# A list schedule's due times, leads and planned lengths are set anew, and five late low halves lie at other addresses

## The chip, the cores and the metric

The kernel runs on one core of one Trainium2 chip. The metric is the device time of one execution in microseconds (us). PE is TensorE (matmul), DVE is VectorE, ACT is ScalarE, POOL is GpSimd, SP is SyncE, which here only issues DMAs.

## The reference

Banded attention over 4 batches, 8 heads, 768 positions and 64 features per head (each position sees the 128 positions up to its own and the first 4), and behind it a feed-forward layer without experts to choose from:

```python
def _attn_ref(q, k, v, n_sink, window):
    scores = (1.0 / np.sqrt(D)) * np.matmul(q, k.transpose(0, 1, 3, 2))
    keep = (pos[None, :] < n_sink) | ((rel >= 0) & (rel < window))      # n_sink 4, window 128
    scores = np.where(keep, scores, -1000000000.0)
    a = np.exp(scores - np.max(scores, axis=-1, keepdims=True))
    a = a / (np.sum(a, axis=-1, keepdims=True) + 1e-09)
    return np.matmul(a, v)

def _moe_ref(x, w_in, w_out):            # x: 3072 x 512, w_in: 512 x 2048, w_out: 2048 x 512
    h = x @ w_in
    g = h - np.tanh(h)
    return g @ w_out
```

All inputs are fp32. The kernel keeps fp32 accuracy by splitting an operand into a high half (rounded to fp32r, which TensorE takes) and a low half (what the rounding left), and adding the products high by high, low by high and high by low.

## The kernel before

**Tiling.** The 3072 tokens are 12 chunks of 256 tokens, the 2048 columns of `w_in` are 8 groups `g` of 256. A pair of chunk and group is a step `n`; there are 96. Steps 0 to 23 are chunks 0 to 2, mixed; from there on step 24 + 8(c − 3) + g is group `g` of chunk `c`, so that a chunk is eight steps in a row. A step is one block of 24 matmuls 128x256 (`mm1`, L823, into `h`), a gate, and a second half. The gate is a tanh on ACT (L843), a difference on DVE (L846), and the split into a high half on ACT and a low half on DVE: L849 (`ghbuf`) and L852 (`glbuf`) in the steps before 40, and L862 and L865, with three more sums on DVE (L857 to L859), from step 40 on. The second half multiplies by `w_out`: 12 matmuls 128x512 at L894 (eight on the high half of the gate, four on the low one), or, in steps 40 to 94, 21 matmuls 128x256 at L928, which are the three passes over seven Strassen products. Their weights (`edge`, and a block in `w`) are made on the chip.

**Attention** is cut into 48 units, four pairs of heads for each chunk. A unit is: scores on PE (L532 in the first chunks, L539 after), the mask and its row maximum on DVE (L554, L556), exponentials on ACT (L564), reciprocals on DVE (L584, L585), scaling on ACT (L590), three small operations for the first four positions on POOL (L599 to L601, `z`), transposes on PE (L624 of `p`, L665 of `z`), merges on DVE (L638), and the products with `v` on PE (L681, L687). The next unit's `q` and `k` are split on ACT and DVE (L508, L511, L497, L502). What comes out is split into `xall` (L704, L708), the operand of `mm1`.

**Weights for the Strassen steps.** `derive(g, m)` makes a sum of two blocks of `w_out`: SP copies the one into place (L1023), POOL starts a DMA that adds the other to it (L1026), ACT rounds the sum to its high half (L1029), DVE leaves the low half (L1036, or L1034 for a negative sum). For `m` = 1, 3, 4 the sum goes into an `edge` tile, in the time of chunk 3's attention; for `m` = 6 it goes into `w` itself, group by group in steps 32 to 39, as soon as the last plain second half has read that block.

**Other DMAs.** The blocks of `w_in` are kept in device memory and streamed back from step 24 on (L808, SP). POOL issues the loads of `q` and `k` (L370, L361) and half of the stores of the result (L985); SP issues the other half.

**What sets the order.** All of this is handed as tasks to a list schedule, `Work`. A task names its engine, a planned length (`took`), a due time, and what it reads and writes; a DMA names in `lands` how long until its data are there. `order()` plays the tasks through, always takes the ready task with the earliest due time, and the instructions are written out in the order that comes out. Each engine then runs its own queue in that order, and waits at an instruction whose inputs aren't there. Due times are made of `due_step(n)` (FIRST, EARLY, PACE) and leads: LEAD3 for chunk 3's attention, LEAD for later chunks, DEAR and DLATE for `derive`, WLEAD and WNEXT for the weights. LAND is added to a DMA's landing:

```python
free[e], done[n] = t + (took if e == "POOL" else lands), t + lands + (1700 if self.all[n][2] < self.late else self.land)
```

Nothing but these numbers decides where in an engine's queue an instruction stands.

**Where low halves lie.** `low7(n)` puts the low half of a Strassen step into a flat buffer, at an offset that is zero but for the steps in a table (`ASIDE`, in words of four bytes; a product's block is 128 words):

```python
def low7(n):
    a = ASIDE.get(n, 0)
    return glflat[:, a : a + 7 * P].rearrange("p (b t) -> p b t", b=7)
```

Of the kernel before, what the change touches and what calls it, by code (L numbers as in the profile page):

```python
# [233 lines left out]
def _banded(tc, qd, kp, vp, vs, small, masks, w_in, w_out, ident, pts, early, out):  # L234
    nc = tc.nc
    et = mybir.EngineType
    with ExitStack() as ctx:
# [16 lines left out]
        banks = {n: ps.tile([P, 512], F32, tag=n, name=n) for n in ("s0", "s1", "o0", "o1", "t", "x")}  # L254
# [9 lines left out]
        kscr = dpool.tile([2, P, 2, DM // 2], F32, tag="kscr", name="kscr")  # L264

        RAW, TWO, CUT, DUO, SC, PB, ZL, TK = 12, 12, 2, 3, 4, 4, -4000, 1100
        SLK, PAD, LATE, LAND, QP, KP, BP, LEAD3 = 0.0, 1.05, 65222.0, 4372.0, 0, 0, 0, 89032.0
        SA, NSLOT, RING, GP, LQ, ST = 5, 7, 7, 0, 1, 1
        work = Work(SLK, PAD, LATE, LAND)

# [4 lines left out]
        order += [(cc, g) for g in range(CUT, NG) for cc in (2, 1)] + [(0, g) for g in range(CUT, NG)]  # L275
        order += [(cc, g) for cc in range(3, NCHUNK) for g in range(NG)]
        NS = len(order)
        FIRST, EARLY, PACE, LEAD = 45000.0, 4600.0, 8242.0, 72963.0
        UNIT, SECOND, WLEAD, WNEXT = 2000.0, 3000.0, 6000.0, 2500.0
        HALF2, LAST = 8269.0, 4401.0  # L280
        SPILL, STREAM, DEAR, DLATE = 54590.0, 4000.0, 39769.0, 31275.0

        def due_step(n):
            return FIRST + EARLY * min(n, 24) + PACE * max(0, n - 24)
# [20 lines left out]
        def shift(n):  # L305
            return SHIFT if n < 24 else 0

        ASIDE = {81: 48, 85: 104, 89: 84, 92: 60}

        def low7(n):  # L310
            a = ASIDE.get(n, 0)
# [624 lines left out]
        def second_half7(n):  # L936
            cc, g = order[n]
            if closes(n):
                runs = [[(m, k) for m in ms for k in range(3)] for ms in ((4, 3), (1,), (2, 5), (7, 6))]
            else:  # L940
                runs = [[(m, k) for m in ms for k in range(2)] for ms in ((4, 3), (1,), (2, 5), (7, 6))]
                runs += [[(m, 2) for m in ms] for ms in ((4, 3, 1), (2, 5, 7, 6))]
            for run in runs:
                def some(run=run):
                    for m, k in run:
                        mm7(n, m, k)

                r = []
                for m, k in run:
                    r.append(("gl", 0) if k == 2 else ("gh", n % 2))  # L950
                    r.append(("e", g, m) if m in (1, 3, 4) else ("w", 1, g))
                banks = {where7[m] for m, _ in run}
                work.add("PE", 119 * len(run), due_step(n) + HALF2, some, sorted(set(r), key=str), sorted(banks))
            if closes(n):
                gather(n)

# [56 lines left out]
        def derive(g, m):  # L1013
# [32 lines left out]
                else:  # L1046
                    src.append(("edge", e))
            took = 300 * n
            work.add("SP", 400, d, copied, src, w + old, lands=took + 100)
            work.add("POOL", 650, d, added, src, w, lands=1000 + 600 * n)  # L1050
            work.add("ACT", 360 * n, d, rounded, (), w)
            work.add("DVE", 360 * n, d, rest_of, (), w, port=True)

# [13 lines left out]
        def first_half(n):  # L1067
            cc, g = order[n]
            if streamed(n):
                for j in range(4):  # L1070
                    work.add("SP", 500, due_step(n) - STREAM + 700 * j, lambda j=j: stream(n, j),
                             [("scr", g, j // 2)], [("ring", ring_at(n, j))] + ([("w", 0, 1)] if cc == 3 and g == 0 else []), lands=850)
            for f in range(2):
                for z in range(2):
                    def some(k0=f * 12 + z * 6):
                        for k in range(k0, k0 + 6):
                            mm1(n, k)

                    x = [("xu", home(cc), 2 * z), ("xu", home(cc), 2 * z + 1), ("x", home(cc))]
                    w = ("ring", ring_at(n, 2 * f + z)) if streamed(n) else ("w", 0, g)  # L1080
                    work.add("PE", 722, due_step(n) - LAST * (n == NS - 1), some, x + [w], [("h", n % 2)])

        def second_half(n):
            if strassen(n):
# [295 lines left out]
```

## Time and profile before

| | |
|---|---|
| device time, three runs | 682.92, 680.07, 674.58 us; median 680.07 |
| the profiled execution | 675.38 us, of it 673.6 from the first to the last instruction |
| busy, of the span | PE 97%, DVE 81%, ACT 59%, POOL 24% |
| mean granted TensorE clock | 0.997 of full |
| instructions | 14515, of them 5099 matmuls |

The three runs spread over 8.3 us, and the profiled execution is near the fastest of them. Matmuls overlap, so that a row of x24 is 24 matmuls that start evenly in the time to the next row's start; a row's own duration reaches into the next.

### The profile page before, as it was taken

The page shows a single profiled execution, that of the slowest core. Times are in us where ns is not written, and L with a number is a line of the kernel's source. Part 1 is how long each engine was busy: PE and PEld are TensorE (multiplying, and loading weights), DVE is VectorE, ACT ScalarE, POOL GpSimd, SP SyncE. Part 2 cuts the span into 40 slices and gives each one's busy share as a digit, 9 for nine tenths or more (in the row PEclk, how much of TensorE's full clock was granted, in tenths as well). Part 3 has the DMA queues.
Part 4 walks back from the last instruction along what each step waited for, and adds up shares of the span by engine and source line. Part 5 has one row for each costly group of instructions (what it writes and reads, how often), then busy time and mean ns, then how long its engine had stood idle before and what let it go on. Part 6 is the DMA issues. An engine that isn't in the chain of part 4 may idle for free.

```text
span 673.6 us, 14515 instructions
## 1 busy us (share of the span) xinstructions
PE 650.5 (97%) x5099; PEld 601.6 (89%) x5099; DVE 543.8 (81%) x1397; ACT 395.8 (59%) x1024; POOL 163.5 (24%) x331
## 2 busy tenths in 40 slices
PE   6899999999999999998999999999999999999995
PEld 4677899989879899897999999899999999999995
DVE  6899998965999877576799899888999889855654
ACT  5986443435887767555675666667566567523331
POOL 5444000002863242232412212222212211100100
PEclk9999999999999999999999999999999999999998
DMA  5878797785989676899977767766776866656861
GB/s 174 282 253 284 271 302 252 290 289 160 217 198 268 205 221 219 241 271 279 253 250 239 222 210 219 240 199 193 238 231 192 263 208 194 216 152 199 260 195 37
DMA packets 79342, 152.97 MB, mean 227 GB/s; under 512 B 9564, under 2 KB 25564, under 8 KB 79260
## 3 DMA queue, kind: packets, MB, share of 16 engines
q1 hardware_dynamic: 65884, 121.65, 57.3%
q0 software_dynamic: 13376, 30.30, 16.4%
q8 instruction: 42, 0.69, 0.4%
q14 instruction: 40, 0.33, 0.2%
HBM read 131.47 MB, written 20.45 MB: 226 GB/s over the span
## 4 chain that ended last, share of the span: by engine, by line
PE 78%; DVE 7%; DMA 4%; ACT 4%; issue 3%; POOL 3%; SPq 0%; POOLq 0%; DVEq 0%; ACTq 0%
PE h L823 32%; PE s L928 10%; PE o L928 8%; PE o L894 7%; PE x L687 3%; PE s L894 3%; PE t L687 2%; DMA w<-bscr 2%; PE t L624 2%; PE t L894 2%; PE x L894 2%; PE t L539 2%; PE x L539 2%; PE s L539 1%; DMA v<-vp 1%
## 5 line engine op out<-in xcount | busy, mean ns | idle before, releaser
L823 PE MATMUL h<-xall,ring 128*128 128x256 f32 x990 | 127.6, 278 | 0.0
L823 PEld LDWEIGHTS h<-xall,ring 128*128 128x128 f32 x990 | 120.1, 188 | 0.9 <-DMA ring<-wscr 0.2
L843 ACT ACTIVATE gbuf<-h 128x512 f32<-128x512 f32 x96 | 57.3, 596 | 98.2 <-PE h L823 71.4
L823 PE MATMUL h<-xall,spare 128*128 128x256 f32 x738 | 96.2, 278 | 0.0
L862 ACT CAST ghbuf<-gbuf 128x896 fp32r<-128x896 f32 x55 | 51.9, 943 | 66.4 <-DVE gbuf L859 66.3
L823 PEld LDWEIGHTS h<-xall,spare 128*128 128x128 f32 x738 | 89.9, 188 | 0.6 <-issue 0.2
L370 POOL DMA_DIRECT2D qraw<-qd x36 | 27.5, 764 | 229.2 <-DVE q L511 181.1
L865 DVE TENSOR_TENSOR glbuf<-gbuf,ghbuf 128x896 fp32r<-128x896 f32 x55 | 59.8, 1088 | 18.8 <-ACT ghbuf L862 16.5
L564 ACT ACTIVATE p<-p,st 128x132 f32<-128x132 f32 x132 | 52.5, 400 | 11.3 <-DVE st L556 10.3
L894 PE MATMUL o<-w,ghbuf 128*128 128x512 f32 x192 | 51.0, 399 | 0.3 <-ACT ghbuf L849 0.3
L846 DVE TENSOR_TENSOR gbuf<-h,gbuf 128x512 f32<-128x512 f32 x55 | 37.8, 688 | 15.2 <-ACT gbuf L843 14.4
L823 PE MATMUL h<-xall,w 128*128 128x256 f32 x384 | 49.3, 279 | 0.0
L823 PEld LDWEIGHTS h<-xall,w 128*128 128x128 f32 x384 | 47.3, 188 | 1.5
L502 DVE TENSOR_TENSOR ks<-kraw,ks 64x392 fp32r<-64x392 f32 x72 | 40.4, 561 | 6.1 <-ACT ks L497 4.0
L590 ACT ACTIVATE p<-p,st 128x132 f32<-128x132 f32 x132 | 42.6, 395 | 4.0 <-DVE st L585 3.6
L894 PEld LDWEIGHTS o<-w,ghbuf 128*128 128x128 f32 x192 | 33.7, 188 | 6.4 <-ACT ghbuf L849 0.8
L497 ACT CAST ks<-kraw 64x392 fp32r<-64x392 f32 x72 | 37.1, 515 | 3.8 <-DMA kraw<-kp 2.9
L846 DVE TENSOR_TENSOR h<-h,gbuf 128x512 f32<-128x512 f32 x41 | 28.5, 696 | 12.8 <-ACT gbuf L843 12.2
L638 DVE TENSOR_TENSOR pt<-t,below 128x512 f32<-128x512 f32 (+1 forms) x48 | 28.8, 599 | 10.7 <-PE t L624 5.7
L928 PE MATMUL o<-w,ghbuf 128*128 128x256 f32 x220 | 35.7, 281 | 0.0
L928 PE MATMUL s<-edge,ghbuf 128*128 128x256 f32 x220 | 35.6, 280 | 0.0
L928 PE MATMUL s<-w,ghbuf 128*128 128x256 f32 x220 | 35.1, 278 | 0.0
(180 smaller groups left out, 1537.7 us busy)
## 6 DMA issues: line engine op xcount, KB each, us to landing
ring<-wscr SPq DMA_DIRECT2D x165, 256.0 KB, 4.5
spare<-wscr SPq DMA_DIRECT2D x123, 256.0 KB, 4.5
qraw<-qd POOLq DMA_DIRECT2D x36, 256.0 KB, 5.1
wraw<-w_in SPq DMA_DIRECT2D x16, 512.0 KB, 6.1
wraw<-w_out SPq DMA_DIRECT2D x16, 512.0 KB, 6.6
wscr<-w SPq DMA_DIRECT2D x16, 512.0 KB, 6.4
kraw<-kp POOLq DMA_DIRECT2D x36, 196.0 KB, 4.3
v<-vp POOLq DMA_DIRECT2D x18, 256.0 KB, 3.7
```

The source lines that it names most:

```text
L497: nc.scalar.copy(ks[u][r, h, :], kt[u][r, :])
L502: (nc.gpsimd if KP else nc.vector).tensor_tensor(k[o, h, :], t[r, :], k[r, h, :].bitcast(F32), op=ALU.subtract)
L539: nc.tensor.matmul(ps[h][:, :WIN], lhsT=q[:, h, t * P : (t + 1) * P], rhs=rhs, start=i == 0, stop=i == 1,)
L564: nc.scalar.activation(e, e, AF.Exp, bias=st[u][:, j : j + 1], scale=-1.0, accum_out=st[u][:, 4 + j : 5 + j],)
L590: nc.scalar.activation(pr[u][:, j, :], pr[u][:, j, :], AF.Copy, scale=s[:, 8 + j : 9 + j])
L823: nc.tensor.matmul(hps[n][:, f, :], lhsT=w, rhs=x, start=r == 0, stop=r == 11)
L843: nc.scalar.activation(g0, h(), AF.Tanh)
L846: nc.vector.tensor_tensor(g0 if strassen(n) else h(), h(), g0, op=ALU.subtract)
L862: nc.scalar.copy(ghbuf[:, n % 2], gbuf[:, 1:, :])
L865: nc.vector.tensor_tensor(low7(n), gbuf[:, 1:, :], ghbuf[:, n % 2].bitcast(F32), op=ALU.subtract)
L894: nc.tensor.matmul(sums_of(n, cc, t), lhsT=a[:, f, t * P : (t + 1) * P], rhs=wt[1, g][:, (0, 1, 0)[i], f, :], start=first and not low and ...
L928: nc.tensor.matmul(acc, lhsT=a[:, b, :], rhs=factor(g, m, part % 2), start=g == 0 and part == 0 and m in (4, 1, 2, 7), stop=closes(n) and ...
```

## The change

Only numbers change. Seventeen of them are due times, leads and the like in the schedule's setting; four more are the landing times planned for the two DMAs of `derive` and the planned lengths of the blocks of matmuls at L823 and L928. They add and remove no instruction; what they change is the order in which engines get them. `ASIDE` changes addresses alone: before, steps 81, 85, 89 and 92 lay at 192, 416, 336 and 240 bytes from the buffer's start; now steps 81, 83, 86, 89 and 92 lie at 336, 240, 336, 240 and 336.

```diff
@@ -264,7 +264,7 @@
-        SLK, PAD, LATE, LAND, QP, KP, BP, LEAD3 = 0.0, 1.05, 65222.0, 4372.0, 0, 0, 0, 89032.0
+        SLK, PAD, LATE, LAND, QP, KP, BP, LEAD3 = 0.0, 1.05, 68932.8, 4939.1, 0, 0, 0, 92253.7
@@ -275,10 +275,10 @@
-        FIRST, EARLY, PACE, LEAD = 45000.0, 4600.0, 8242.0, 72963.0
-        UNIT, SECOND, WLEAD, WNEXT = 2000.0, 3000.0, 6000.0, 2500.0
-        HALF2, LAST = 8269.0, 4401.0
-        SPILL, STREAM, DEAR, DLATE = 54590.0, 4000.0, 39769.0, 31275.0
+        FIRST, EARLY, PACE, LEAD = 45488.2, 4498.8, 8248.4, 74582.8
+        UNIT, SECOND, WLEAD, WNEXT = 2182.8, 6399.4, 6045.8, 1426.5
+        HALF2, LAST = 8288.8, 5144.0
+        SPILL, STREAM, DEAR, DLATE = 62388.8, 3653.6, 44193.8, 26553.2
@@ -305,7 +305,7 @@
-        ASIDE = {81: 48, 85: 104, 89: 84, 92: 60}
+        ASIDE = {81: 84, 83: 60, 86: 84, 89: 60, 92: 84}
@@ -950,7 +950,7 @@
-                work.add("PE", 119 * len(run), due_step(n) + HALF2, some, sorted(set(r), key=str), sorted(banks))
+                work.add("PE", 123.7 * len(run), due_step(n) + HALF2, some, sorted(set(r), key=str), sorted(banks))
@@ -1046,8 +1046,8 @@
-            work.add("SP", 400, d, copied, src, w + old, lands=took + 100)
-            work.add("POOL", 650, d, added, src, w, lands=1000 + 600 * n)
+            work.add("SP", 400, d, copied, src, w + old, lands=took + 552)
+            work.add("POOL", 650, d, added, src, w, lands=2054 + 600 * n)
@@ -1078,7 +1078,7 @@
-                    work.add("PE", 722, due_step(n) - LAST * (n == NS - 1), some, x + [w], [("h", n % 2)])
+                    work.add("PE", 739, due_step(n) - LAST * (n == NS - 1), some, x + [w], [("h", n % 2)])
```

With LAND, the planned time from the issue of a `derive(g, 6)` copy to its landing goes from 700 + 4372 = 5072 ns to 1152 + 4939 = 6091 ns, that of its addition from 2200 + 4372 = 6572 to 3254 + 4939 = 8193 ns.

The order moves at these places of which the rows tell. In names such as `h_3649` the number is the program's count of tiles and differs between the two kernels for the same thing.

**Steps 39 and 40, ACT.** `h_3649` before and `h_3653` now are the first product of step 39, `h_3722` and `h_3732` that of step 40, `w_4` is the block of group 4 that `derive(4, 6)` makes, `p_3737` and `p_3713` are the same attention unit. Before:

```order
L1029 ACTIVATE w_3_1213<-w_3_1213 128x512
L590 ACTIVATE p_3591<-p_3591,st 128x132 x4
L843 ACTIVATE gbuf<-h_3649 128x512
L1029 ACTIVATE w_4_1330<-w_4_1330 128x512
L849 CAST ghbuf<-h_3649 128x512
L564 ACTIVATE p_3737,nswi<-p_3737,nswi 128x132 x2
L843 ACTIVATE gbuf<-h_3722 128x512
```

Now:

```order
L1029 ACTIVATE w_3_1193<-w_3_1193 128x512
L843 ACTIVATE gbuf<-h_3653 128x512
L849 CAST ghbuf<-h_3653 128x512
L564 ACTIVATE p_3713,nswi<-p_3713,nswi 128x132 x2
L508 CAST q_3743<-qraw_3636 128x512
L1029 ACTIVATE w_4_1298<-w_4_1298 128x512
L564 ACTIVATE p_3713,nswi<-p_3713,nswi 128x132 x2
L497 CAST ks_3772<-kraw_3687 64x392 x2
L590 ACTIVATE p_3713<-p_3713,nswi 128x132 x4
L843 ACTIVATE gbuf<-h_3732 128x512
```

The rounding of `w_4` stood ahead of the gate's high half (L849); now it stands behind it, behind the first two of the unit's exponentials (L564), and ahead of the other two, which the scaling (L590) needs.

**The same place, PE.** `t` and `x` are the two banks into which the scores (L539) go, `o` is the sum of the second half. Before, and then now:

```order
L539 MATMUL t<-ks_3628,q_3626 128x260 x2
L539 MATMUL x<-ks_3628,q_3626 128x260 x2
L823 MATMUL h_3722<-xall,ring 128x256 x18
L823 MATMUL h_3722<-xall,spare 128x256 x6
L539 MATMUL t<-ks_3628,q_3626 128x260 x2
L539 MATMUL x<-ks_3628,q_3626 128x260 x2
L894 MATMUL o_252<-w_7_1603,ghbuf 128x512 x4
```

```order
L894 MATMUL o_252<-w_6_1522,glbuf 128x512 x2
L894 MATMUL o_253<-w_6_1522,glbuf 128x512 x2
L539 MATMUL t<-ks_3638,q_3620 128x260 x2
L539 MATMUL x<-ks_3638,q_3620 128x260 x2
L823 MATMUL h_3732<-xall,ring 128x256 x18
L823 MATMUL h_3732<-xall,spare 128x256 x6
L894 MATMUL o_252<-w_7_1597,ghbuf 128x512 x4
L894 MATMUL o_253<-w_7_1597,ghbuf 128x512 x4
L624 MATMUL t<-ident,p_3713 128x128 x4
L894 MATMUL o_252<-w_7_1597,glbuf 128x512 x2
```

The second pair of scores stood behind the block of 24 matmuls; now it stands ahead of it, and behind the block comes, after eight matmuls of L894, the transpose (L624) of that unit's `p`.

**Steps 20 and 21, DVE.** `h_1991` before and `h_1988` now are the first product of step 21, `p_2158` and `p_2147` the same unit of chunk 3's attention. Before:

```order
L638 TENSOR_TENSOR pt<-t,below 128x4x128
L638 TENSOR_TENSOR pt<-t,after 128x4x128
L554 COPY_PREDICATED s_250<-above,s_250 128x128
L556 ISA p_2158,nswi<-s_250,mask 128x132
L556 ISA nswi 128x1
L554 COPY_PREDICATED s_251<-above,s_251 128x128
L556 ISA p_2158,nswi<-s_251,mask 128x132
...
L852 TENSOR_TENSOR glbuf<-h_1991,ghbuf 128x512
L511 TENSOR_TENSOR q_2189<-qraw_2113,q_2189 128x512
L584 TENSOR_SCALAR nswi<-nswi 128x4
```

Now:

```order
L511 TENSOR_TENSOR q_2086<-qraw_2005,q_2086 128x512
L502 TENSOR_TENSOR ks_2095<-kraw_2030,ks_2095 64x392 x2
L584 TENSOR_SCALAR st<-st 128x4
L585 RECIPROCAL st<-st 128x4
L852 TENSOR_TENSOR glbuf<-h_1988,ghbuf 128x512
L1034 SCALAR_TENSOR_TENSOR edge_1802<-edge_1802 128x256
L554 COPY_PREDICATED s_250<-above,s_250 128x128
L556 ISA p_2147,nswi<-s_250,mask 128x132
L556 ISA nswi 128x1
L554 COPY_PREDICATED s_251<-above,s_251 128x128
L556 ISA p_2147,nswi<-s_251,mask 128x132
```

The low half of step 21 (L852) stood behind both groups of that unit's masks (the group shown here is the second) and the merges L638 between them; now it stands ahead of all of them.

**POOL at 430 us.** `z` are the three operations for the first positions, `out` the store of a finished chunk. Before, and then now:

```order
L601 CAST z<-z 128x2x16
L985 DMA out<-wide 128x512
L985 DMA out<-wide 256x1x256
L599 CAST z<-p_5169 128x2x8
L600 TENSOR_TENSOR z<-p_5169,z 128x2x8
L601 CAST z<-z 128x2x16
L370 DMA qraw_5278<-qd 128x2x256
L361 DMA kraw_5326<-kp 128x392
```

```order
L370 DMA qraw_5186<-qd 128x2x256
L599 CAST z<-p_5123 128x2x8
L600 TENSOR_TENSOR z<-p_5123,z 128x2x8
L601 CAST z<-z 128x2x16
L985 DMA out<-wide 128x512
L985 DMA out<-wide 256x1x256
L361 DMA kraw_5299<-kp 128x392
```

The two stores stood ahead of `z`; now they stand behind it. The same exchange is made once more, at the unit whose `z` runs at 586 us.

## Rows read from the trace of the kernel before

**Rows 1.** The page: busy time of PE and DVE, and the granted clock by fortieths.
```profile
PE 650.5 (97%) x5099; PEld 601.6 (89%) x5099; DVE 543.8 (81%) x1397; ACT 395.8 (59%) x1024; POOL 163.5 (24%) x331
PEclk9999999999999999999999999999999999999998
```

**Rows 2.** Waits of PE: who waited for what, us in total, times, longest.
```profile
PE t L539 <- DVE nswi L556: 2.5, 1, 2.5
...
PE t L894 <- ACT ghbuf L849: 1.6, 2, 0.9
PE o L894 <- DVE glbuf L852: 1.6, 2, 1.3
...
PE x L665 <- POOL z L601: 0.8, 2, 0.6
```

**Rows 3.** Windows of 40 us: length, busy of PE, PEld, DVE, ACT, POOL, clock, DMA share, GB/s.
```profile
160.00:200.00 40.00, 38.12 (x279) 33.31 (x278) 35.71 (x114) 32.09 (x98) 28.47 (x44) 1.00 0.93 209
...
280.00:320.00 40.00, 37.48 (x251) 33.94 (x250) 27.16 (x77) 22.73 (x63) 12.02 (x20) 1.00 0.99 276
...
400.00:440.00 40.00, 39.37 (x357) 38.01 (x356) 36.51 (x96) 25.77 (x64) 10.32 (x21) 1.00 0.73 235
```

**Rows 4.** Timeline of PE at 318 us: start, us, instruction, idle before and releaser.
```profile
318.60 0.51 PE L539 MATMUL t<-ks,q 128*128 128x260 f32 x2 [2.48 <-DVE nswi L556]
```

**Rows 5.** Timeline of ACT from there.
```profile
315.94 0.63 ACT L1029 ACTIVATE w<-w 128x512 fp32r<-128x512 f32 x1 [5.63 <-DMA w<-bscr]
...
320.51 0.52 ACT L497 CAST ks<-kraw 64x392 fp32r<-64x392 f32 x1
320.93 0.40 ACT L564 ACTIVATE p<-p,nswi 128x132 f32<-128x132 f32 x1
...
323.86 1.30 ACT L590 ACTIVATE p<-p,nswi 128x132 f32<-128x132 f32 x4
```

**Rows 6.** DMA issues of `derive(g, 6)`: count, KB, median us from issue to landing.
```profile
w<-bscr SPq DMA_DIRECT2D x8, 256.0 KB, 4.8
w<-bscr POOLq DMA_DIRECT2D x8, 256.0 KB, 8.0
```

**Rows 7.** Timeline: the issues for group 4, on SP and on POOL.
```profile
299.45 0.37 SPq L1023 DMA_DIRECT2D w<-bscr  x1
307.93 1.22 POOL L1026 DMA_DIRECT2D w<-bscr  x1 [8.93 <-PE h L823]
```

**Rows 8.** Timeline of PE and DVE: low half of step 21, then that of 24.
```profile
187.76 1.20 PE L894 MATMUL o<-w,glbuf 128*128 128x512 f32 x4 [1.30 <-DVE glbuf L852]
187.02 0.69 DVE L852 TENSOR_TENSOR glbuf<-h,ghbuf 128x512 fp32r<-128x512 f32 x1
208.56 0.69 DVE L852 TENSOR_TENSOR glbuf<-h,ghbuf 128x512 fp32r<-128x512 f32 x1
210.16 2.02 PE L894 MATMUL o<-w,ghbuf 128*128 128x512 f32 x8
```

**Rows 9.** Timeline of POOL and PE at 430 us.
```profile
429.25 1.27 POOL L985 DMA_DIRECT2D out<-wide  x2 [8.40 <-DVE wide L980]
431.55 0.44 PE L665 MATMUL x<-ident,z 128*128 128x128 f32 x2 [0.63 <-POOL z L601]
```

**Rows 10.** The chain that ended last, late steps: start, us, what.
```profile
600.88 2.83 PE h L823 x24
606.18 2.83 PE h L823 x24
...
643.12 2.72 PE h L823 x24
648.22 2.72 PE h L823 x24
```

**Rows 11.** Timeline: the high half of step 48, and PE's first use of it.
```profile
376.08 0.95 ACT L862 CAST ghbuf<-gbuf 128x896 fp32r<-128x896 f32 x1
377.66 0.62 PE L928 MATMUL s<-edge,ghbuf 128*128 128x256 f32 x4
```

## The prediction

> **What bounds the kernel now.** The page comes first: PE is busy for 97% of the span, DVE for 81%, and the granted clock is full but at the end [rows 1]. So the time is PE's work, which this change leaves as it is, plus the moments in which PE stands still, plus the pace at which PE takes matmuls. The list of PE's waits tells what there is to win [rows 2]: 2.5 us once for scores that wait for a mask on DVE, 3.2 us for the high and low halves of gates, 0.8 us for POOL's `z`. The rest of PE's idle time is start and tail, and in both the order stays: the first seven gates have the same DVE work ahead of them, and the last hundred instructions of PE, DVE and ACT are the same. The windows say in which stretch the waits lie [rows 3]: 160 to 200 us, where DVE works 35.7 of 40 us, and 280 to 320, where DVE works only 27.2 of 40 but the DMA share is 0.99. The first stretch is short of DVE, the second waits for a transfer. In the window of 400 to 440 DVE is at 36.5 of 40: there the next bound lies close.
>
> **Part 1: the stall at 316 us.** After the block of step 40 PE starts the next scores at 318.60, with 2.48 us idle ahead of them [rows 4]. Behind it stands ACT, held until 315.94 by the DMA that adds into `w` [rows 5]; in DVE's queue the low half of that weight waits for ACT, and the gate's low half and the masks wait behind it. The copy was issued at 299.45, the addition at 307.93 [rows 7], so copy and addition took 315.94 − 299.45 = 16.5 us, where the medians of the eight are 4.8 and 8.0 [rows 6]. The new order takes the gate and the first masks out from behind the weight, so this wait of 2.5 us goes. What is late next? ACT now does, after the addition has landed: the weight (0.63 us, of which the next instruction overlaps some 0.1), the other two exponentials (each some 0.4 with a read behind it, 0.9 together), two casts of 0.52, and the scaling, 1.30 [rows 5]; then the transpose L624 can start. That is 0.5 + 0.9 + 1.0 + 1.3 + 0.2 for the signal = 3.9 us behind the landing, or 0.2 + 16.5 + 3.9 = 20.6 us behind the end of the pass that frees the block. In the new order PE has between that pass and this transpose 72 matmuls of 256 columns at 2.72/24 = 0.113 us [rows 10], 36 of 512 columns at twice that, 16 scores at 0.12 and four short ones: 8.2 + 8.2 + 1.9 + 0.3 = 18.6 us. If this transfer is as slow as before, 2.0 of the 2.5 us come back as a wait in front of the transpose: 0.5 us is won. If copy and addition take their medians (14.1 us with the 1.3 us that now lie between the copy's landing and the addition's issue, an estimate), none comes back: 2.5 us. The bounds are 0.5 and 2.5; I take 0.8, near the lower, since the row is of this very transfer and the DMA share of the stretch, 0.99 [rows 3], gives no reason for a quicker one.
>
> **Part 2: the gates of chunk 3's attention.** PE waits there twice for a low half, the longer time until 187.76 [rows 8], and once for a high half; from the starts of its matmuls the three cost 2.4 us. At 187.02 DVE starts on the half that PE wants [rows 8], and its row shows no idle time ahead: it wasn't waiting for data, it came late from its queue. Multiplying each row of the order by the mean time of such a row in the trace, DVE has 3.4 us less ahead of the low half of step 20 and 4.8 us less ahead of step 21's, and PE's work ahead of both is the same. The longest of these waits is 1.3 us [rows 2], so all of them should go: 2.4 us. The work isn't gone; it stands ahead of step 24 now, with 2.7 us more on DVE and 0.9 more on PE. There the low half was ready at 208.56 + 0.69 = 209.25, and PE came to it behind eight matmuls that began at 210.16 [rows 8], at 0.23 each: 2.8 us later. With PE 2.4 us earlier, 2.7 − 0.9 + 2.4 = 4.2 us would be asked for, if DVE never found time to catch up: up to 1.4 us of new wait for the low half. DVE has about 4.3 us free in the 40 [rows 3], so I take 0.9 of it. Sum of the part: 1.5 us, between −0.5 (step 24 late by more than counted) and 2.4.
>
> **Part 3: POOL's stores.** At 429.25 POOL starts two stores, 1.27 us long, then does `z`, and PE, which had waited 0.63 us for it, goes on at 431.55 [rows 9]. With `z` ahead of the stores, the issues fall away in front of it, more than PE's wait. The like holds at 586 us with 0.2 us. Matmul starts put the two waits at 1.16 us; I take the 0.8 of the list [rows 2]. The stores go out 1 us later, and nobody reads them. If `z` then waits for `p` on ACT, the win is nothing: 0 to 1.2 us.
>
> **Part 4: the addresses.** With the clock full, PE has two paces in the last 80 us. Steps with nothing but 24 + 21 matmuls follow each other every 606.18 − 600.88 = 5.30 us, and later every 648.22 − 643.12 = 5.10 us; their blocks of 24 take 2.83 and 2.72 us [rows 10]. The slow pace begins with the low half of step 81 (at 192 bytes from the buffer's start) and ends with that of step 89 (336 bytes); step 92's (240 bytes) is slow itself, and the pace after it is full. Eight steps at 0.20 us make 1.6 us. The change keeps just the two offsets after which the pace was full. Should they keep it so throughout, 1.6 us are won; should each such step merely turn the pace over, then steps 81 to 83, 86 to 89 and 92 to 95 are slow, eight again, and nothing is won; should all steps from 81 on be slow, 14 × 0.2 = 2.8 us are lost in place of 1.6: −1.2. I take 1.0, nearer to the first, because 336 and 240 bytes were each followed by the full pace the one time they occur, while no row shows them after a full pace.
>
> Here a rule speaks against the change. The Trainium skill, "SBUF — State Buffer", "Who interferes with whom", gives PE a read port for the moving operand and one for the weights, and says that PE never waits on anyone there; by it an address would move nothing. The trace has two paces at one clock, which that rule alone doesn't explain, and doesn't show that the address is their cause. By the rule the sum would be 1.0 us smaller.
>
> **Part 5: the rest.** From 340 to 595 us units and gates are interleaved anew. Counted as in part 2, DVE's work ahead of the gates of steps 41 to 64 grows against PE's by 1.4 to 2.7 us, and by 4.5 at step 48. The schedule sends PE to a gate just when it is ready: step 48's high half ends at 377.03 and PE uses it at 377.66, 0.63 us later [rows 11]. Where DVE has its results early the growth costs nothing; I take 0.4 us of new waits, between 0 and 4.
>
> **Sum.** 0.8 + 1.5 + 0.8 + 1.0 − 0.4 = 3.7 us less than the profiled execution of 675.38: 671.7, a ratio of 0.9945. The profiled execution lies 4.7 us under the median of the runs, 680.07; the forecast is for a median, so 680.07 × 0.9945 = 676.4 us.
>
> **The rivals.**
> *The waits only move.* The transfer of group 4 comes back in full as a wait of the transpose, step 24 is late by 1.4 us, and the pace turns over as before: 0.5 + 1.0 + 0.8 − 2 from part 5 = about 0.3 us, 679.8. For it speaks that three of the five parts have the next late thing in sight; against it that parts 2 and 3 win on engines that the rows show late by their own queue.
> *The address is nothing* (the skill's rule above): as forecast without part 4, 2.7 us, which gives 677.4.
> *DVE becomes the bound behind 340 us.* The place is step 48. If DVE, at 36.5 of 40 us in such a stretch [rows 3], has no time in hand, PE waits 4.5 − 0.6 = 3.9 us there, and with the 1.4 us of step 24 in full and the slow pace kept from step 81 on (−1.2) the sum is 0.8 + 1.0 + 0.8 − 1.2 − 3.9 = −2.5 us: 682.6, slower than before. It decides from the point where DVE is more than 4 us later at that gate than its slack. Against it: DVE's idle tenths are spread over the stretch, and one wait of PE gives all later gates the same time.
> *Everything works*: 2.5 + 2.4 + 1.2 + 1.6 = 7.7 us, which gives 672.3.
>
> **How the numbers follow.** Forecast 0.38, waits only move 0.2, address nothing 0.14, DVE the bound 0.15, everything 0.13. 2% of this time is 13.6 us, about what a measurement of this kernel can tell from no change; all the cases lie inside it. A few in a hundred stay for each side: faster 0.04 (a shorter chain nobody counted), same 0.93, slower 0.03. The range reaches from the case in which everything works, 672.3, less half of the runs' own spread to their lowest (5.5/2 = 2.7), to the case with DVE as the bound: 669.6 to 682.5.
>
> **What would show it.** Part 1: the wait of the scores at 316 us is gone, and a wait of L624 for L590 stands 3 us later, 0 to 2 us long. Part 2: no wait of L894 between 170 and 190 us, perhaps one at step 24. Part 3: no waits for `z`. Part 4: blocks of 24 at 2.72 us from 595 to 658. Part 5: new waits of L928 for L862 of 0.4 us in sum. I am wrong if PE's waits in sum are not about 3 us less, or if they are and the time is not.

## The result, and the profile after

| | before | changed |
|---|---|---|
| first comparison, median | 680.15 us (4 runs, 674.58 to 682.92) | 670.3 us (4 runs, 669.1 to 671.8) |
| ratio, 95% interval | | 0.9889 [0.9851, 0.9927] |
| second comparison, median | 677.66 us (23 runs, 674.32 to 680.1) | 669.29 us (6 runs, 668.91 to 671.75) |
| ratio, 95% interval | | 0.9878 [0.9853, 0.9902] |
| profiled execution | 675.38 us, span 673.6 | 669.1 us, span 667.3 |

The changed kernel is 1.1% to 1.2% faster by the recorded ratios (the two medians alone would give 0.9855 and 0.9877). The forecast was 676.4 us, a ratio of 0.9945, with a range from 669.6 to 682.5: the way is right, and the first comparison's time, 670.3, lies in the range, at its edge; the second's, 669.29, lies 0.3 us under it. The gain was about twice what was forecast (1.1% to 1.2% against 0.55%). The two profiled executions differ by 6.3 us, where the forecast's sum was 3.7. The same parts of the page as in [rows 1], of the changed kernel: busy time of each engine, and the granted clock by fortieths.

```profile
PE 649.1 (97%) x5099; PEld 601.1 (90%) x5099; DVE 543.9 (82%) x1397; ACT 396.8 (59%) x1024; POOL 164.9 (25%) x331
PEclk9999999999999999999999999999999999999999
```

The work is the same: each engine's count of instructions stands as it was (the page's total, 14542 against 14515, differs by semaphore instructions alone). What differs is how long PE stands still. Its waits in the changed kernel, as in [rows 2] (us in total, times, longest):

```profile
PE s L532 <- DMA qk<-qd: 2.3, 2, 1.7
PE x L681 <- ACT zr L672: 1.7, 2, 0.9
...
PE t L894 <- DVE glbuf L852: 0.8, 1, 0.8
...
PE o L894 <- ACT ghbuf L849: 0.2, 1, 0.2
PE t L539 <- DVE pt L638: 0.2, 1, 0.2
```

None of the four waits of [rows 2] stands there with its old size: the scores' wait for `nswi` is gone, the halves of gates are down from 3.2 us to 0.2 (0.8 more, for the step that ends the program, stood in the list before as well), and POOL's `z` is gone. New is L681, which waits for ACT's `zr`. Without the 3.2 us of the start, which are in both lists, the waits of this list sum to 13.2 us before and 8.6 now: 4.6 of the 6.3 us. The windows of [rows 3] now:

```profile
160.00:200.00 40.00, 39.24 (x281) 34.41 (x280) 36.31 (x116) 34.53 (x104) 28.09 (x46) 1.00 0.92 205
...
280.00:320.00 40.00, 40.00 (x274) 36.59 (x273) 32.48 (x90) 28.91 (x79) 15.52 (x26) 1.00 0.99 295
...
400.00:440.00 40.00, 40.00 (x365) 38.96 (x364) 36.50 (x96) 25.27 (x66) 10.49 (x22) 1.00 0.73 221
```

PE's busy time goes from 38.12 to 39.24, from 37.48 to 40.00 and from 39.37 to 40.00. In the second window the DMA share is 0.99 as before: the transfers are as crowded, and PE no longer waits for them. The chain that ended last shows PE's pace, late steps as in [rows 10]:

```profile
595.88 2.72 PE h L823 x24
601.02 2.73 PE h L823 x24
```

A block of 24 takes 2.72 us where it took 2.83, and a step 5.12 us on average (from 590.77 to 652.25, twelve steps) where it took 5.30. Over the eight slow steps of before that is 1.4 us. 4.6 and 1.4 make 6.0, but they don't close the account, because the slow pace is not confined to the last steps. In the changed kernel it stands ahead of step 81 too, for example here:

```profile
397.78 2.83 PE h L823 x24
```

Counted from the starts of the matmuls of 256 columns at L823 and L928, from 335 us to the low half of step 81, 267 of 1815 follow each other at the slow pace (116 to 126 ns) in the kernel before and 488 of 1784 in the changed one, which loses 0.9 us by it. From that low half on it is 380 of 592 before and 41 now, 1.5 us won. So over the whole execution the pace gives some 0.5 us, and the rest of the 6.3 is in stops of PE, of which the list names 4.6.

### The profile page after: what moved, and what is told of

The parts are those of the page before. It is cut to its first block, busy times and chain, and to the rows that moved or that the text cites. A ratio compares the mean times of both kernels' runs of the same rounds, so it can differ in the third digit from the quotient of the medians.

```text
span 667.3 us, 14542 instructions
## 1 busy us (share of the span) xinstructions
PE 649.1 (97%) x5099; PEld 601.1 (90%) x5099; DVE 543.9 (82%) x1397; ACT 396.8 (59%) x1024; POOL 164.9 (25%) x331
## 3 DMA queue, kind: packets, MB, share of 16 engines
q0 software_dynamic: 13376, 30.30, 16.2%
## 4 chain that ended last, share of the span: by engine, by line
PE 85%; DVE 5%; ACT 4%; DMA 2%; POOL 2%; issue 1%; POOLq 0%; SPq 0%; DVEq 0%; ACTq 0%
PE h L823 36%; PE s L928 11%; PE o L894 8%; PE o L928 8%; PE x L687 3%; PE s L894 3%; PE t L687 2%; PE t L624 2%; PE t L539 2%; PE t L894 2%; PE x L539 2%; PE x L894 2%; PE s L539 1%; DMA ring<-wscr 1%; DVE pt L638 1%
## 5 line engine op out<-in xcount | busy, mean ns | idle before, releaser
L823 PE MATMUL h<-xall,ring 128*128 128x256 f32 x990 | 130.4, 279 | 0.0
L823 PEld LDWEIGHTS h<-xall,ring 128*128 128x128 f32 x990 | 121.2, 188 | 1.4 <-issue 0.7
L823 PE MATMUL h<-xall,spare 128*128 128x256 f32 x738 | 97.5, 278 | 0.0
L823 PEld LDWEIGHTS h<-xall,spare 128*128 128x128 f32 x738 | 90.8, 188 | 0.5
L865 DVE TENSOR_TENSOR glbuf<-gbuf,ghbuf 128x896 fp32r<-128x896 f32 x55 | 59.9, 1089 | 20.2 <-ACT ghbuf L862 17.2
L564 ACT ACTIVATE p<-p,st 128x132 f32<-128x132 f32 x132 | 52.4, 399 | 12.2 <-DVE st L556 11.2
L894 PE MATMUL o<-w,ghbuf 128*128 128x512 f32 x192 | 50.3, 397 | 0.2 <-ACT ghbuf L849 0.2
L823 PEld LDWEIGHTS h<-xall,w 128*128 128x128 f32 x384 | 46.8, 188 | 2.1 <-DVE w L751 0.5
L823 PE MATMUL h<-xall,w 128*128 128x256 f32 x384 | 48.1, 279 | 0.3 <-DVE w L751 0.3
L590 ACT ACTIVATE p<-p,st 128x132 f32<-128x132 f32 x132 | 42.6, 395 | 3.6 <-DVE st L585 3.1
L894 PEld LDWEIGHTS o<-w,ghbuf 128*128 128x128 f32 x192 | 33.8, 188 | 6.4 <-ACT ghbuf L849 0.5
L846 DVE TENSOR_TENSOR h<-h,gbuf 128x512 f32<-128x512 f32 x41 | 28.5, 696 | 13.2 <-ACT gbuf L843 12.8
L849 ACT CAST ghbuf<-h 128x512 fp32r<-128x512 f32 x41 | 24.0, 586 | 21.1 <-DVE h L846 20.4
L928 PE MATMUL s<-edge,ghbuf 128*128 128x256 f32 x220 | 35.2, 279 | 0.0
L928 PE MATMUL o<-w,ghbuf 128*128 128x256 f32 x220 | 35.1, 278 | 0.0
L928 PE MATMUL s<-w,ghbuf 128*128 128x256 f32 x220 | 35.0, 278 | 0.0
```

What stands on the lines that cost most here:

```text
L564: nc.scalar.activation(e, e, AF.Exp, bias=st[u][:, j : j + 1], scale=-1.0, accum_out=st[u][:, 4 + j : 5 + j],)
L590: nc.scalar.activation(pr[u][:, j, :], pr[u][:, j, :], AF.Copy, scale=s[:, 8 + j : 9 + j])
L823: nc.tensor.matmul(hps[n][:, f, :], lhsT=w, rhs=x, start=r == 0, stop=r == 11)
L846: nc.vector.tensor_tensor(g0 if strassen(n) else h(), h(), g0, op=ALU.subtract)
L865: nc.vector.tensor_tensor(low7(n), gbuf[:, 1:, :], ghbuf[:, n % 2].bitcast(F32), op=ALU.subtract)
L894: nc.tensor.matmul(sums_of(n, cc, t), lhsT=a[:, f, t * P : (t + 1) * P], rhs=wt[1, g][:, (0, 1, 0)[i], f, :], start=first and not low and ...
```

## The experiments

Times are compared with the kernel before on the same chip. All edits are made to one of the two kernels; where a schedule's number is edited, the whole order follows.

### e1: the kernel before again

No edit. 

> The kernel before, unchanged, with a second profile. The medians differ by 9.8 us (680.15 to 670.3) where the two profiled executions differ by 6.3. Theory A (the stall at 316 us hangs on a transfer whose length varies): the second profile is some us longer than the first, 677 to 681, and the excess stands in the waits behind the DMA that adds into w, at 300, 316 and 336 us. Rival B (the slow pace of PE comes and goes): the excess is in stretches where blocks of 24 take 2.83 us. Rival C (the first profile is typical and the runs differ by chance): 673 to 677, no new wait.

Measured: 676.06 us against 677.79 for the same kernel, ratio 0.9974 [0.9948, 1.0]. So a ratio here can be off by 0.3%, which is 1.8 us, without cause. The second profile is 677.35 us long. Timelines of its ACT (start, us, idle before and releaser) and of PE at the place of [rows 4] and [rows 5]:

```profile
315.74 0.63 ACT L1029 ACTIVATE w<-w 128x512 fp32r<-128x512 f32 x1 [2.37 <-DMA w<-bscr]
```

```profile
306.16 0.51 PE L539 MATMUL t<-ks,q 128*128 128x260 f32 x2 [0.77 <-DVE st L556]
327.59 0.44 PE L665 MATMUL x<-ident,z 128*128 128x128 f32 x2 [0.46 <-POOL z L601]
```

The copy for group 4 was issued at 301.28 there, so ACT's rounding started 14.5 us later, where it took 16.5 in the first profile. The 2.48 us of PE at this place are gone, and smaller waits stand before and behind. In two more kernels with the order of before at this place, e2 and e10 below, the same took 17.2 and 17.0 us, and PE waited 3.25 and 3.02 us. So the stall does hang on a transfer whose length varies by 2.7 us from one execution to the next, as theory A had it.

Behind the two longer stalls something more is lost. In e2, PE's first matmuls after the stall, and the granted clock from there (a window as in [rows 3], of PE alone):

```profile
320.92 3.17 PE L894 MATMUL o<-w,ghbuf 128*128 128x512 f32 x8
320.00:323.40 3.40, 3.40 (x10) 0.50 0.95 241
```

The clock is at 0.50 of full, the level of 1.2 GHz, for 3.4 us, in e10 too. In the first profile it stayed at 1.00 behind the 2.48 us. From the scores to the gate's low half PE takes 4.2 us in e2 and 4.1 in e10, where it took 2.75: 1.3 to 1.4 us more.

The second profile of e1 is longer for the same reason at another place. The scores (L532) behind a wait near 18 us, in the first profile and then in e1, and the clock there in e1:

```profile
17.80 1.11 PE L532 MATMUL s<-qk 128*128 128x260 f32 x4 [2.19 <-DVE nswi L556]
18.22 2.07 PE L532 MATMUL s<-qk 128*128 128x260 f32 x4 [2.35 <-POOL z L600]
18.00:21.40 3.40, 3.18 (x11) 0.50 0.64 199
```

PE comes there 0.4 us later than in the first profile, and by 41 us it is 1.8 us later, nearly all of the 1.9 us by which the spans differ; the waits listed up to 45 us are no longer than in the first profile. Theory A is right on the mechanism, and wrong on this profile, where the stall at 316 us is gone; the slow pace of rival B was there as before and added nothing. What is longer is a stretch at half clock, which none of the three had.

### e2 and e3: the addresses alone, the order alone

```diff
 e2, the kernel before:
-        ASIDE = {81: 48, 85: 104, 89: 84, 92: 60}
+        ASIDE = {81: 84, 83: 60, 86: 84, 89: 60, 92: 84}
 e3, the changed kernel:
-        ASIDE = {81: 84, 83: 60, 86: 84, 89: 60, 92: 84}
+        ASIDE = {81: 48, 85: 104, 89: 84, 92: 60}
```

> The kernel before with nothing changed but the offsets of the low halves (steps 81, 83, 86, 89, 92 at 336, 240, 336, 240, 336 bytes). Theory (the address of a low half sets the pace that follows): blocks of 24 take 2.72 us from 595 to 658, the time falls by 1.6 us. Rival (the offsets do nothing, the pace comes from the order of instructions): the slow steps stay, change under 0.3 us. Rival (the offsets make most of the gain): 6 us or more less.

> The changed kernel with the offsets of before (steps 81, 85, 89, 92 at 192, 416, 336, 240 bytes). Theory: 1.6 us above the changed kernel, that is about 672 against 670.3, with blocks of 24 at 2.83 us from step 82 to 89. Rival (offsets do nothing): 670.3. Rival (offsets are most of it): 676 or more.

Measured: e2 677.0 us, ratio 0.999 [0.9967, 1.0013]; e3 671.61 us, 0.9921 [0.9896, 0.9946]. The chain of e2, then of e3:

```profile
603.40 2.72 PE h L823 x24
...
645.00 2.83 PE h L823 x24
...
655.62 2.73 PE h L823 x24
```

```profile
596.52 2.83 PE h L823 x24
...
638.74 2.72 PE h L823 x24
```

From step 81 on the addresses set the pace: with the new ones the old order runs at 2.72 us where it had 2.83, and with the old ones the new order falls back to 2.83 from step 82 to step 89. In e3 the twelve steps from the first full block on take 62.86 us, 1.4 more than in the changed kernel. In e2 the pace is lost again ahead of step 89's second half and comes back with step 92, at 336 bytes; about 0.9 us are won there, which the ratio can't tell from none. Most of the gain is the order's: e3 has it without the addresses.

### e4: only the stall at 316 us

```diff
+        later(made[4, 6, "DVE"], 3)      # in the order as written out: three DVE tasks later
+        later(made[4, 6, "ACT"], 2)
```

> The kernel before with two instructions moved: ACT's rounding of group 4's weight goes behind the gate's high half and the first two exponentials, DVE's low half of it behind that unit's masks. Theory (the stall at 316 us ends where it was, without coming back): PE's wait of 2.5 us is gone, 2.5 to 3 us less. Rival (as the prediction took it, 2.0 us come back at the next wait for ACT): 0.5 us less. If the transfer is longer in most runs than in the first profile, the gain in the median is larger, 4 us or more.

Measured: 674.42 us, ratio 0.9965 [0.9945, 0.9985], which is 2.4 us (1.0 to 3.7). Timelines of ACT and PE:

```profile
316.47 0.63 ACT L1029 ACTIVATE w<-w 128x512 fp32r<-128x512 f32 x1 [1.05 <-DMA w<-bscr]
```

```profile
324.16 0.73 PE L928 MATMUL s<-edge,ghbuf 128*128 128x256 f32 x4 [0.48 <-ACT ghbuf L862]
```

The rounding starts as late as ever (the copy was issued at 299.85, so 16.6 us), but now only 1.05 us of ACT's time are lost to it, PE's scores don't wait, and 0.5 us come back at the gate of step 40. Two instructions moved by hand give nearly a third of the whole gain. The interval takes in the 1.8 us by which e1 was off without cause, so the profile's lines, 2.5 us of wait gone and 0.5 back, carry this verdict more than the ratio does.

### e5: only the gates of steps 20 and 21

```diff
+        sooner(lows[20], 2)      # two DVE tasks earlier: ahead of both merges L638
+        sooner(lows[21], 3)      # three: ahead of both merges and a group of masks
```

> The kernel before with DVE's low halves of steps 20 and 21 (L852 there, L854 in this kernel) taken ahead of the two merges L638 and the masks that stood before them. Theory (DVE came late from its queue): the waits at 178.7 and 187.8 us go, 1.5 to 2 us less in 160 to 200. Rival (the work that is now behind is late in its turn, at the next scores or transposes): PE loses the same time up to 30 us later, under 0.5 us less in the window from 160 to 215.

Measured: 677.15 us, 0.9994 [0.9969, 1.002]. PE's waits from 186 to 200 us:

```profile
191.43 0.33 PE L624 MATMUL t<-ident,p 128*128 128x128 f32 x1 [0.23 <-ACT p L590]
192.02 0.62 PE L624 MATMUL t<-ident,p 128*128 128x128 f32 x3 [0.26 <-ACT p L590]
193.73 0.44 PE L665 MATMUL x<-ident,z 128*128 128x128 f32 x2 [0.60 <-POOL z L601]
```

The waits for low halves, 0.3 us at 178.7 and 1.3 at 187.8 [rows 8], are gone, and the masks that now stand behind them make the unit's scaling and `z` late: 1.1 us in these lines, and 0.15 more at a high half ahead of them. The rival is right: under 0.5 us is left. Where DVE works 9 of 10 us, one task taken forward is another put back.

### e6: only POOL's stores

```diff
+        for cc in (6, 9):
+            for t in (1, 0):
+                later(stores[cc, t], 1)      # behind the next z
```

> The kernel before with POOL's two pairs of stores of the chunks that end at 429 and 583 us put behind the next z. Theory: both waits of PE for z go, 0.8 to 1.2 us less, nothing else. Rival (z then waits for p, or the stores hold up the next loads): no gain, or new waits behind 430 and 586 us.

Measured: 677.73 us, 1.0011 [0.9979, 1.0042], which can't tell 0.7 us from none. The profile can. POOL and PE at the place of [rows 9]:

```profile
432.10 0.24 POOL L599 CAST z<-p 128x16 fp32r<-128x16 f32 x1 [9.25 <-ACT p L590]
```

```profile
433.29 0.44 PE L665 MATMUL x<-ident,z 128*128 128x128 f32 x2 [0.36 <-POOL z L601]
```

`z` now waits for ACT's `p`, as the rival said, and PE waits 0.36 us where it waited 0.63; the wait at 586 us is gone. Together 0.5 us of the 0.8. (The order of the changed kernel makes this exchange at a third place too, the stores of 531 us in the kernel before, where PE hadn't waited.)

### e7 and e12: the landing times alone, and everything but them

```diff
 e7, the kernel before (in e12 the changed kernel has the - lines instead):
-        ... LATE, LAND, ... = ... 65222.0, 4372.0, ...
+        ... LATE, LAND, ... = ... 68932.8, 4939.1, ...
-            work.add("SP", 400, d, copied, src, w + old, lands=took + 100)
-            work.add("POOL", 650, d, added, src, w, lands=1000 + 600 * n)
+            work.add("SP", 400, d, copied, src, w + old, lands=took + 552)
+            work.add("POOL", 650, d, added, src, w, lands=2054 + 600 * n)
```

> The kernel before with nothing changed but LATE, LAND and the two landing times planned for derive; the order follows. In it group 4's rounding stands behind the gate, step 21's low half ahead of that unit's masks, and POOL's stores ahead of z as before. Theory (the schedule's idea of these transfers is what matters, all other numbers little): the stalls at 187 and 316 us go, 4 to 6 us less, 672 to 674 where the kernel before has 678. Rival (the gain needs all numbers searched together): about the time of before, with new waits elsewhere.

> The changed kernel with LATE, LAND and derive's two landing times of before; the order follows. In it, too, group 4's rounding stands behind the gate. Theory (the numbers work together, and those of the landings alone are not what counts): no stall at 316 us, but new waits elsewhere, 1 to 4 us above the changed kernel. Rival (the landing times are what made the gain): the stalls of before return, 676 or more.

Measured: e7 676.03 us, 0.9991 [0.9968, 1.0015]; e12 676.56 us, 0.998 [0.996, 1.0001]. PE's waits in e7, then in e12:

```profile
194.24 0.44 PE L665 MATMUL x<-ident,z 128*128 128x128 f32 x2 [0.89 <-POOL z L601]
...
209.95 0.97 PE L823 MATMUL h<-xall,ring 128*128 128x256 f32 x6 [1.14 <-DMA ring<-wscr]
214.24 1.20 PE L894 MATMUL o<-w,glbuf 128*128 128x512 f32 x4 [0.97 <-DVE glbuf L852]
```

```profile
221.02 1.73 PE L894 MATMUL o<-w,glbuf 128*128 128x512 f32 x4 [1.82 <-DVE glbuf L852]
...
309.60 0.33 PE L624 MATMUL t<-ident,p 128*128 128x128 f32 x1 [0.95 <-ACT p L590]
```

In e7 the stalls of 187 and 316 us are gone as foretold, but not the 4 to 6 us with them: waits of 0.6 to 1.1 us for `z`, `xall`, the ring and a gate's low half come up between 194 and 214 us. In e12, with all the other numbers of the change, the low half waits 1.8 us at 221 and the transposes 0.95 at 309.6. So neither the landing times nor the rest have the gain by themselves: 0.1% and 0.2%, against 1.2% together. e12 came out 7 us above the changed kernel where the theory had 1 to 4, and by time where its rival had it; but the stall of 316 us is not back, so the rival's reason is not the right one. The list of PE's waits has 3.1 us more than the changed kernel's (11.7 against 8.6, without the start), and behind the wait at 221 us the granted clock is 0.50 from 221.4 to 224.8 us, at most 1.7 us more; the other 3 us of the 8 between the two profiles are not placed.

### e8, e10 and e11: offsets of zero, and one offset

```diff
 e8, the changed kernel, and e10, the kernel before:
+        ASIDE = {}
 e11, the changed kernel:
+        ASIDE = {81: 84}
```

> The changed kernel with every low half at offset zero. Theory (an offset resets the pace, and without one a slow pace stays until something disturbs it): the changed kernel comes to step 81 at the slow pace, so blocks of 24 take 2.83 us from step 82 to the end, 14 steps at 0.2: 2.5 to 2.8 us above the changed kernel. Rival (offsets themselves cause the slow pace, zero is best): 2.72 us throughout, no slower than the changed kernel. Rival (offsets do nothing): the same pace as in the changed kernel.

> The kernel before with every low half at offset zero. Its PE comes to step 81 at the full pace. Theory (a low half at 192 bytes turns the pace slow, one at zero leaves it as it is): without the offset of step 81 blocks of 24 take 2.72 us from step 82 on, until another disturbance, at step 88 or later; 1 to 2 us less lost from 595 to 640. Rival (the slow pace begins at step 81 whatever lies there): 2.83 us from 595 to the end, 1.2 us more lost than before.

> The changed kernel with only the first of its five offsets, step 81 at 336 bytes. Theory (336 bytes resets a slow pace once, the others hardly matter): as the changed kernel to step 88, within 0.3 us there; if steps 88 and 89 disturb the pace, up to 1.4 us slower behind them. Rival (each offset holds the pace for a few steps only): slow again within four steps of 81, 2 us above the changed kernel.

Measured: e8 672.43 us, 0.9935 [0.9912, 0.9959]; e10 676.65 us, 0.9975 [0.9952, 0.9998]; e11 669.95 us, 0.9882 [0.9848, 0.9915]. The chains of e8, e10 and e11:

```profile
596.38 2.83 PE h L823 x24
601.68 2.83 PE h L823 x24
...
654.68 2.83 PE h L823 x24
```

```profile
603.72 2.72 PE h L823 x24
...
645.03 2.83 PE h L823 x24
```

```profile
602.71 2.72 PE h L823 x24
...
653.76 2.72 PE h L823 x24
```

All three went the way the theory had it. In e8 every step from 82 on is slow, 5.30 us each, and from the first full block to the last 63.60 us go by where the changed kernel takes 61.48: 2.1 us over these twelve steps, near the 2.5 to 2.8 foretold for fourteen. The medians lie 2.1 and 3.1 us apart (672.43 against 670.3 and 669.29, from other comparisons). In e10 the old order, which comes to step 81 at the full pace, keeps it through step 88, where it was slow at the offset of before: 192 bytes had turned it. It falls inside the block ahead of step 89's second half, behind a stop of PE of 0.2 us (in e2, at the same place, of 0.4), and is slow to the end, since nothing turns it back. In e11 one offset of 336 bytes at step 81 is enough: from there to the end every block takes 2.72 us, and the twelve steps take 61.27. The other four offsets of the change aren't needed in that profile; by time e11 and the changed kernel can't be told apart. No version tried is clearly faster than the changed kernel.

### e9: the changed kernel again

No edit. 

> The changed kernel, unchanged, timed once more beside the kernel before, with a second profile. The first comparison gave 0.9889 [0.9851, 0.9927], where the kernel before had a median of 680; in the experiments so far it had 677.7. Theory (PE's waits and pace as read from the profiles: five profiles of the order of before lost 28.3 to 30.5 us, the changed kernel 21.8, so 6.5 to 8.8 us): ratio 0.988 to 0.991, 670 to 671. Rival (part of the first comparison was the chip or chance): ratio over 0.992.

Measured: 669.29 us, 0.9878 [0.9853, 0.9902]: the gain is there again in a second comparison. The second profile, at 671.75 us the longest of its six runs, shows the place of the old stall with a slower transfer: SP's issue, ACT, and PE.

```profile
299.64 0.37 SPq L1023 DMA_DIRECT2D w<-bscr  x1
```

```profile
315.88 0.63 ACT L1029 ACTIVATE w<-w 128x512 fp32r<-128x512 f32 x1 [1.21 <-DMA w<-bscr]
...
318.27 1.29 ACT L590 ACTIVATE p<-p,nswi 128x132 f32<-128x132 f32 x4
```

```profile
318.73 0.33 PE L624 MATMUL t<-ident,p 128*128 128x128 f32 x1
319.32 0.62 PE L624 MATMUL t<-ident,p 128*128 128x128 f32 x3 [0.26 <-ACT p L590]
```

The transfer takes 16.2 us, 0.3 less than in [rows 5] and [rows 7], and PE loses 0.3 to 0.5 us to it where it had lost 2.5. Of the 2.65 us by which this profile is longer than the first, some 1.5 come with a stretch at a granted clock of 0.50, from 19.6 to 23.0 us, as in e1.

## Why the prediction was right, and where its sizes were off

**What bounds the kernel** held: the work is the same, and the gain is in PE's stops, of which the list names 4.6 us, and in PE's pace behind step 81 (1.4 us). What the sum left out is the pace ahead of step 81, which costs 0.9 us, and the granted clock, which was full in the one profile at hand [rows 1] and is not in every execution.

**Part 1 was mis-sized, 0.8 us where e4 measures 2.4 (1.0 to 3.7) and the profiled pair 2.5.** That the wait of the scores would go was right. That "2.0 of the 2.5 us come back as a wait in front of the transpose" was wrong. In the first profile of the changed kernel:

```profile
297.88 0.37 SPq L1023 DMA_DIRECT2D w<-bscr  x1
```

```profile
313.11 0.63 ACT L1029 ACTIVATE w<-w 128x512 fp32r<-128x512 f32 x1 [0.19 <-DMA w<-bscr]
...
315.49 1.30 ACT L590 ACTIVATE p<-p,nswi 128x132 f32<-128x132 f32 x4
```

```profile
316.78 0.60 PE L624 MATMUL t<-ident,p 128*128 128x128 f32 x4
```

the transfer took 15.2 us and no wait stands at the transpose; with 16.2 us, in e9, 0.3 to 0.5 us do. The step that failed is the chain behind the landing. I let the transpose wait for the whole scaling, 1.3 us and 0.2 for the signal (that 0.2 is in no row: in [rows 8] PE starts 0.05 us behind the end of the low half it waited for). The row with x4 is four instructions, and four transposes follow them one by one: the first started 0.46 us after the first scaling (318.27, 318.73). That is 1.0 us of the 2.0. PE's own work up to there was 19.1 us from the copy's issue (299.64 to 318.73) where I had counted 18.6 from the pass that ends 0.2 us ahead of it: 0.5 to 0.7 us more. The rest is the transfer's 0.3. e4 puts the part by itself at 2.4 us.

**Part 2 was right in sum by luck.** From 160 to 220 us PE's waits fell from 1.9 us (two low halves, one high) to 1.0:

```profile
193.64 0.50 PE L681 MATMUL x<-zr,vsink 128*128 128x512 f32 x1 [0.76 <-ACT zr L672]
...
208.68 2.13 PE L894 MATMUL o<-w,ghbuf 128*128 128x512 f32 x8 [0.23 <-ACT ghbuf L849]
```

The second row is step 24, where a wait was foretold: it is one for the high half, not the low one, and 0.2 us long. The first is one I hadn't named. So 0.9 us came where 1.5 were forecast. Not foreseen was that a wait of 0.78 us for a high half at 150 us goes too in the new order; only with it are there 1.7 us. e5 shows that the local step I argued with, less work ahead of two gates, is worth nothing that can be measured by itself. That the rest of the new order puts what is moved where nobody waits is argued from the lists of waits, and no run shows it by itself.

**Part 3** was right in the profile: 0.8 us forecast, and no wait for `z` is left. The exchange of stores and `z`, made at 430 and 586 us, is made at a third place as well (e6). POOL's stores come behind `z`, whose user runs before them (POOL, then PE):

```profile
424.66 1.28 POOL L985 DMA_DIRECT2D out<-wide  x2 [0.99 <-DVE wide L980]
```

```profile
424.23 0.38 PE L665 MATMUL x<-ident,z 128*128 128x128 f32 x2
```

**Part 4** was right for the steps it counts and a little small: 1.0 forecast, 1.4 us measured with e3. It took the two paces for a matter of the last 80 us; ahead of step 81, where all low halves lie at zero, the changed kernel is slow more often than the kernel before. The bound of 1.6 (the pace is full after each offset) was the case that held, and the bound by which each such step should "merely turn the pace over" fell. What e8, e10 and e11 add is the cause: at step 81 the pace follows the address. The rival's rule, in the Trainium skill, "SBUF — State Buffer", "Who interferes with whom", says that PE reads the moving operand and the weights through ports of their own and waits on no other engine. It doesn't speak of addresses; that by it an address would move nothing was the prediction's inference, and that doesn't hold here: e8 and the changed kernel differ in nothing but offsets, and by 2.1 us.

**Part 5** was near in its waits: 0.4 us of new ones forecast; the list has 0.2 behind 340 us. The 0.9 us that the pace loses in the same stretch were not foreseen. The rival of DVE as the bound fell at its place, step 48 (ACT, then PE):

```profile
369.97 0.95 ACT L862 CAST ghbuf<-gbuf 128x896 fp32r<-128x896 f32 x1
```

```profile
372.16 0.62 PE L928 MATMUL s<-edge,ghbuf 128*128 128x256 f32 x4
```

The high half is ready at 370.92, 1.2 us before its use, where it was 0.6 [rows 11]. The count of 4.5 us seems to have taken that gate at its old place in the order; no run tests that.

**From one execution to the median.** The profiled pair has a ratio of 0.9907, the second pair (677.35 and 671.75) 0.9917, the comparisons 0.9878 and 0.9889. So about 2 us of the gain are in neither pair. The mean granted clock that is on record for each run points to where they are. Of the 79 runs of the kernel before beside the experiments, 20 have a mean clock of 0.996 or more and a median of 675.2 us; the other 59 have a median of 678.1. Of the changed kernel's ten runs, seven have 0.996 or more, with 669.3 us, and three less, with 671.8. Among the runs of higher clock the ratio of the medians is 0.991, as in the profiled pairs: what the medians add goes with the kernel before losing clock more often. In the traces a stretch at half clock stands behind the longer stalls of 316 us (e2, e10), which the new order no longer has, and near 20 us in both orders (e1, e5, e6, e9, e11). That the runs without a trace lose their clock at the same places is argued and not shown, and the mean also counts the clock of the idle end.

## What to carry to other kernels

Before a wait is said to come back at the next user, count the chain by single instructions: a row of x4 is four, and its readers may start behind the first. In a stretch where an engine works 9 of 10 us, moving one task forward by hand moves the wait to what was put back (e5), and the numbers of a whole order can work only together (e7, e12). Before a spread of times is put down to one wait, set each run's time beside its mean granted clock. And where blocks of like matmuls take two different times at the same granted clock, try another address for the operand of the step at which the pace changes.

## What the hardware showed that I had not expected

PE has two paces at a granted clock of 1.00: a block of 24 matmuls takes 2.72 or 2.83 us, 113 or 118 ns for one. It keeps a pace until something turns it, here for up to fourteen steps. The address of the operand that L928 loads as weights turns it: a low half at 192 bytes from the buffer's start turned the full pace slow (in the kernel before, e1 and e4), one at 336 bytes turned the slow pace full (before, changed, e11, and e2 at step 92) and left the full one as it was (e2 at step 81), and one at zero left either as it was (e8, e10). Other things turn it too: in e2 and e10 it fell behind a stop of 0.4 and 0.2 us inside a block, and ahead of step 81 both paces come with all low halves at zero. Why an address does this, no run here shows.

The granted clock fell from 1.00 to 0.50 (from 2.4 to 1.2 GHz) for 3.4 us just behind waits of PE of 3.25 us (e2), 3.02 (e10) and 1.8 (e12), where a wait of 2.48 us in the kernel before left it at 1.00. So the length of the wait alone doesn't tell here whether the clock falls.

The transfer of 256 KB for group 4, a copy and an addition into the same place, took 14.5 to 17.2 us from the copy's issue to ACT's start in the order of before, with nothing changed about it, in a stretch where the DMA share is 0.99.
